# Attention and a two-layer product on one core: a first token range of 640 and all token blocks in pairs

## The chip, the core and the metric

The kernel runs on one core of a Trainium2 chip. A core has a matrix engine (TensorE, "PE" in the profile; its weight loads are "PEld"), a vector engine (VectorE, "DVE"), a scalar engine with activation functions (ScalarE, "ACT"), a general engine (GpSimd, "POOL"), and SyncE ("SP"), which here only issues DMA transfers. Each engine takes its instructions in order. The metric is the device time of one execution in microseconds (us). Three executions of the kernel before took 394.09, 394.75 and 396.04 us.

## The reference, cut to what matters

```python
# q, k, v: (8 batches, 12 heads, 448 tokens, 64); w_in: (768, 2048); w_out: (2048, 768)
scores = (1 / sqrt(64)) * q @ k.T            # per batch and head
attn = exp(scores - max(scores)); attn /= sum(attn) + 1e-9
x = attn @ v                                 # heads side by side: (3584 tokens, 768)
h = x @ w_in
g = maximum(0.01 * h, h)
out = g @ w_out                              # (3584, 768) float32
```

## The kernel before

**Units.** Two heads of one batch are a unit: u = 0 to 47, six to a batch. A unit's q, k and v are loaded (the loads of two units together, through POOL's DMA queue), cast to bf16 by POOL (`cast`; q and k into one of three `qkb` buffers, v into a ring `v_sb` of NV = 5), and q and k are transposed: by PE with a DVE copy for u < NPE = 12 (`transposes`, L248 and L254), by a DMA transposition from SP for the others (`dma_transposes`, L231). `scores` (L265) makes a chunk of 112 keys by 448 queries for two heads; ACT takes its exponential (`expo`, L274); there are four chunks a unit, 192 in all, issued in bursts of three. `rows` (L738) multiplies a whole unit's exponentials by v, the sum of weights coming from a column of ones; DVE takes the reciprocal (L744) and multiplies (L745), giving x. x is transposed into the ring `xT`, by PE for the units of the first batch (u < NXP = 6, L305), by DMA for the others (`x_transposes`).

**Ranges of tokens.** The rest, w_in, activation and w_out, goes by ranges of tokens: 384, 512, 384, 512 and so on, eight ranges cut at the multiples of 128 below the ends of the batches. Range 0 goes plainly through w_in (`plain`, L339: 16 groups of six matmuls; activation at L614) and its tokens go block by block straight through w_out (`blocks`, L586: one block kept for later, two processed). Range 1 is also plain through w_in. From range 2 on `hidden` (L449) uses seven half-size products in place of eight (sums and differences of the halves of x and w_in, and of the partial results), and from range 1 on `block_pair` (L521) does the same for two blocks of 128 tokens at a time and w_out. The sums and differences of the weights are made once, by DVE: `mix_w_in` (L371) and `mix_weights` (L350 to L357); those of x by `mix_x_part` (L396), those of the activations by `mix_h` (L421, L422).

**Order.** The order on every engine is the order in which the program emits. `place` keeps a small model of time (when PE is, when ACT is done, which of the three score slots is free) and puts bursts and rows between the groups of matmuls; how many bursts a stage gets is set by `plan`, `early` and `goals`. During the first two ranges `feed` issues, after each burst, the casts, loads and DMA transpositions that come next, and two of the four pieces of w_out; the others and those of w_in are issued by `supply` and at fixed places of the start. The loads of the weights and of the units go through the same queue, in this order. Later `advance` issues them, one of each kind per step. `mix_weights` and `mix_w_in` are generators: each `next(...)` puts one DVE operation in place.

The steps that matter below: the loads (L132, L176), the casts (L161, L163), the DMA transpositions (L231), scores (L265), rows and x (L738 to L745), the matmuls of w_in in the first range (L339), the DVE operations on the weights (L350 to L357, L371), and the blocks (L586).

Of the kernel before, what the change touches and what calls it, by code (L numbers as in the profile page):

```python
# [16 lines left out]
def kernel(  # L17
# [9 lines left out]
    nc = tc.nc  # L27
# [13 lines left out]
    cuts = [((b * S) // P) * P for b in range(B)] + [B * S]  # L41
# [10 lines left out]
    r_pool = ctx.enter_context(tc.tile_pool(name="rec", bufs=4))  # L52
# [24 lines left out]
    NV = 5  # L77
# [12 lines left out]
    NX = 4 * S  # L90
# [77 lines left out]
    for i in range(4):  # L168
        at = (slice(None), ts(i % 2, MD // 2), ts(i // 2, NW))
        w_steps.append((w_out_sb[at], w_out_v[at]))  # L170
# [56 lines left out]
    NXP = 6  # L227
    NPE = 12
# [12 lines left out]
    def transposes(u, bank=None):  # L241
        if u >= min(NPE, NU):
            return
        for parts in ((1,), (0,)) if u == 0 else ((0, 1),):
            tr = turn_tile(bank)
            for i in parts:
                for so in range(NSC):
                    nc.tensor.transpose(  # L248
                        tr[:, i, ts(so, SC)], qk_sb[u][:, i, so], ident[:SC, :SC]
                    )  # L250
            if u == 0:
                stay_warm(5)
            at = slice(parts[0], parts[-1] + 1)
            (nc.scalar.copy if u == 0 and parts == (0,) else nc.vector.tensor_copy)(  # L254
                qkT[u % NQ][:, :QL].rearrange("p (i s) -> p i s", i=2)[:, at], tr[:, at]
            )
# [39 lines left out]
    def x_transposes(u, bank=None):  # L296
        b, hp = divmod(u, HP)
        at = b * S % NX
        dst = xT[:, hp, at:at + S]
        if u >= NXP:  # L300
            turn(dst, x_t.pop(u).rearrange("p so h d -> p (so h d)"))
            return
# [28 lines left out]
    def part(i, m, kks, bank=None):  # L331

        n = cuts[i + 1] - cuts[i]
        at = cuts[i] % NX
# [9 lines left out]
    def mix_weights():  # L344
# [3 lines left out]
        for lo, hi in pieces:  # L348
            t2, t3, t4 = (w_mix[:, x, lo] for x in range(3))
            nc.vector.tensor_sub(t3, w_out_sb[:, hi, right], w_out_sb[:, lo, right])  # L350
            yield
            nc.vector.tensor_add(t2, t3, w_out_sb[:, lo, left])
            yield
            nc.vector.tensor_sub(t4, w_out_sb[:, hi, left], t2)
            yield
        for lo, hi in pieces:
            nc.vector.tensor_sub(w_out_sb[:, lo, right], w_out_sb[:, lo, right], w_out_sb[:, lo, left])  # L357
            yield
# [24 lines left out]
    def mix_x_part(i, ks):  # L383

        at = cuts[i] % NX
# [13 lines left out]
    def spots(i):  # L399

        n = cuts[i + 1] - cuts[i]
        if n == 4 * P:
            return 0, [(0, 2), (1, 3)]
        if i == 0:
            return 2, []
        return (0, [(0, 1), (KEEP, 2)]) if i % 4 == 2 else (2, [(2, 3)])

    def token(i, x):

        if x == KEEP:  # L410
            return cuts[i - i % 4] + 2 * P
        return cuts[i] + (x - spots(i)[0]) * P
# [11 lines left out]
    def hidden(i):  # L424
# [3 lines left out]
        at = cuts[i] % NX  # L428
# [75 lines left out]
    def block_pair(i, c):  # L504
# [30 lines left out]
        keep(o1, left, b, nc.scalar.copy if c == 0 and (short or i + 1 == B) else nc.vector.tensor_copy)  # L535
# [39 lines left out]
    def blocks(i, todo):  # L575

        o = {}
        for c, w in todo:
            if c not in o:
                o[c] = o_pool.tile([P, DM], F32, name="o")  # L580
            ps = next_bank()
            nw = w.stop - w.start
            for m in range(MD):
                if m == MD // 2:
                    yield MD // 2 * nw, False
                nc.tensor.matmul(  # L586
                    ps[:, :nw], h[:, m, ts(c, P)], w_out_sb[:, m, w],
                    start=(m == 0), stop=(m == MD - 1),
                )
            nc.vector.tensor_copy(o[c][:, w], ps[:, :nw])  # L590
            t0 = token(i, c)
            if w.stop == DM:
                store(o.pop(c), t0)
            yield MD // 2 * nw, True

    def plain(i, sums):

        n = cuts[i + 1] - cuts[i]
        start = spots(i)[0]
        hs = h[:, :, start * P:start * P + n]  # L600
        ready = []
        if i == 0:
            for m in opened:
                part(i, m, (KD - 1,))
        for x in range(MD):
            m = x if i == 0 else x // 2 + x % 2 * MH
            if i > 0 and x == 0:
                for y in (m, m + MH):
                    part(i, y, range(KD - 1))
            if i > 0 and x < 2:  # L610
                part(i, m, (KD - 1,))
            elif m not in opened or i > 0:
                part(i, m, range(KD))
            nc.scalar.activation(hs[:, m], open_t.pop(m)[:, :n], AX.Prelu, alpha=0.01)  # L614
            settle()
            if i == 0:
                if m == opened[-1]:
                    slots.append(idle)
                if m > MD // 2:
                    next(sums)  # L620
            else:
                if ready:
                    mix_h(i, ready.pop())
                if x % 4 == 3:
                    ready.append(x // 2 - 1)
                next(sums)
            yield n
        if ready:
            mix_h(i, ready.pop())
# [295 lines left out]
```

## Time and profile before

| | us |
|---|---|
| median of three executions (394.09 to 396.04) | 394.75 |
| the profiled execution: its own time | 394.7 |
| its span, first to last instruction | 392.8 |
| PE busy in the span | 379.9 (97%) |
| ACT busy | 262.4 (67%) |
| DVE busy | 222.0 (57%) |
| POOL busy | 143.7 (37%) |
| moved by DMA | 47.76 MB, 122 GB/s in the mean |

The durations used in this document come from the profiled execution, whose time lies 0.05 us under the median; 1.9 us of it lie around the span. A matmul's busy time in the profile is longer than the distance to the next one, since matmuls overlap; where PE is full, the distance between starts is what counts. "Releaser" is what an engine's idle time ended with. The row of tenths shows the busy share in 40 equal slices, 9.8 us each.

### The profile page before, as it was taken

The page shows a single profiled execution, that of the slowest core. Times are in us where ns is not written, and L with a number is a line of the kernel's source. Part 1 is how long each engine was busy: PE and PEld are TensorE (multiplying, and loading weights), DVE is VectorE, ACT ScalarE, POOL GpSimd, SP SyncE. Part 2 cuts the span into 40 slices and gives each one's busy share as a digit, 9 for nine tenths or more (in the row PEclk, how much of TensorE's full clock was granted, in tenths as well). Part 3 has the DMA queues.
Part 4 walks back from the last instruction along what each step waited for, and adds up shares of the span by engine and source line. Part 5 has one row for each costly group of instructions (what it writes and reads, how often), then busy time and mean ns, then how long its engine had stood idle before and what let it go on. Part 6 is the DMA issues. An engine that isn't in the chain of part 4 may idle for free.

```text
span 392.8 us, 9958 instructions
## 1 busy us (share of the span) xinstructions
PE 379.9 (97%) x4060; PEld 255.0 (65%) x4060; DVE 222.0 (57%) x476; ACT 262.4 (67%) x401; POOL 143.7 (37%) x222
## 2 busy tenths in 40 slices
PE   7999997699999999999999999999999999999996
PEld 3666664255456598556975569669856696668854
DVE  3662442277567557573475645665746457473754
ACT  5998765367767758776777767877776678608700
POOL 8787643567544433574412355052103000000000
PEclk9999999899999999999999999999999999999999
DMA  8999999999978895999872889549017420131022
GB/s 131 196 200 205 197 179 189 124 201 157 139 108 137 145 162 98 103 209 141 158 94 47 158 124 183 75 102 180 3 31 156 99 67 2 55 89 57 2 73 88
DMA packets 99325, 47.76 MB, mean 122 GB/s; under 512 B 55888, under 2 KB 95952, under 8 KB 99280
## 3 DMA queue, kind: packets, MB, share of 16 engines
q0 software_dynamic: 40272, 22.58, 44.6%
q1 hardware_dynamic: 58944, 24.53, 31.4%
q8 instruction: 31, 0.51, 0.5%
q14 instruction: 14, 0.11, 0.1%
q10 hardware_dynamic: 64, 0.02, 0.0%
HBM read 45.61 MB, written 11.01 MB: 144 GB/s over the span
## 4 chain that ended last, share of the span: by engine, by line
PE 80%; DMA 13%; POOL 5%; issue 1%; DVE 1%; POOLq 0%; DVEq 0%
PE g L521 31%; PE g L449 12%; PE sc L449 12%; PE sc L738 10%; PE sc L265 8%; DMA fv<-in_v_dram 6%; PE g L339 5%; DMA qkT<-qkb 3%; DMA w_mix<-in_v_dram 2%; DMA w_in_mix<-in_v_dram 2%; POOL v L163 1%; PE g L586 1%; POOL w_in_mix L132 1%; POOL qkb L161 1%; POOL w_mix L132 1%
## 5 line engine op out<-in xcount | busy, mean ns | idle before, releaser
L274 ACT ACTIVATE e<-sc 112x896 bf16<-112x896 f32 x192 | 163.1, 920 | 51.2 <-PE sc L265 51.2
L521 PEld LDWEIGHTS <-h 128*128 128x128 bf16 x632 | 57.3, 98 | 44.4 <-issue 12.3
L521 PE MATMUL g<-w_out_sb,h 128*128 128x384 bf16 x416 | 77.7, 326 | 0.0
L265 PE MATMUL sc<-qkT 64*128 64x448 bf16 x384 | 49.7, 353 | 6.9 <-DMA qkT<-qkb 5.7
L161 POOL COPY qkb<-fq 112x512 bf16<-112x512 bf16 x38 | 28.4, 748 | 73.9 <-DMA qkT<-qkb 53.4
L438 ACT ACTIVATE h<-c 128x384 bf16<-128x384 f32 (+1 forms) x72 | 40.6, 575 | 22.0 <-DVE c L464 15.0
L449 PEld LDWEIGHTS <-w_in_sb 128*128 128x128 bf16 x576 | 52.0, 98 | 3.9
L738 PEld LDWEIGHTS <-e 112*128 112x128 bf16 x1344 | 46.4, 98 | 9.0 <-ACT e L274 6.9
L738 PE MATMUL sc<-v,e 112*128 112x65 bf16 x1344 | 49.9, 194 | 0.0
L163 POOL COPY v<-fv 112x512 bf16<-112x512 bf16 x38 | 24.6, 652 | 62.5 <-PE sc L738 33.5
L449 PEld LDWEIGHTS <-w_in_mix 128*128 128x128 bf16 x432 | 39.1, 98 | 2.4
L744 DVE RECIPROCAL rec<-sc 112x8 f32<-112x8 f32 x42 | 8.7, 207 | 55.9 <-PE sc L738 55.8
L521 PE MATMUL g<-w_mix,h 128*128 128x384 bf16 (+1 forms) x208 | 38.7, 323 | 0.0
L339 PE MATMUL g<-xT,w_in_sb 128*128 128x512 bf16 (+1 forms) x180 | 37.9, 355 | 0.0
L526 DVE COPY o<-g 128x384 f32<-128x384 f32 x47 | 26.0, 554 | 18.5 <-PE g L521 17.8
L265 PEld LDWEIGHTS <-qkT 64*128 64x128 bf16 x384 | 14.8, 94 | 33.0 <-issue 19.1
L161 POOL COPY qkb<-fk 112x512 bf16<-112x512 bf16 x38 | 24.5, 645 | 21.2 <-DMA fk<-in_k_dram 18.9
L745 DVE TENSOR_TENSOR x<-sc,rec 112x512 bf16<-112x512 f32 x42 | 29.0, 691 | 1.5
L529 DVE TENSOR_TENSOR o<-o,g 128x384 f32<-128x384 f32 x39 | 21.4, 550 | 13.6 <-PE g L521 13.5
L339 PEld LDWEIGHTS <-w_in_sb 128*128 128x128 bf16 x192 | 17.1, 98 | 17.8 <-issue 4.3
L449 PE MATMUL g<-xT,w_in_sb 128*128 128x192 bf16 (+1 forms) x216 | 26.6, 259 | 0.0
L449 PE MATMUL sc<-xT,w_in_sb 128*128 128x192 bf16 (+1 forms) x216 | 26.6, 259 | 0.0
(94 smaller groups left out, 460.0 us busy)
## 6 DMA issues: line engine op xcount, KB each, us to landing
fq<-in_q_dram POOLq DMA_DIRECT2D x19, 224.0 KB, 5.9
fk<-in_k_dram POOLq DMA_DIRECT2D x19, 224.0 KB, 6.3
fv<-in_v_dram POOLq DMA_DIRECT2D x19, 224.0 KB, 6.2
w_in_sb<-in_moe_w_in_dram POOLq DMA_DIRECT2D x4, 768.0 KB, 11.2
w_out_sb<-in_moe_w_out_dram POOLq DMA_DIRECT2D x4, 768.0 KB, 15.8
out_dram<-o SPq DMA_DIRECT2D x7, 336.0 KB, 5.0
out_dram<-o SPq DMA_DIRECT2D x8, 288.0 KB, 3.8
out_dram<-o SPq DMA_DIRECT2D x7, 240.0 KB, 3.1
```

What stands on the lines that cost most here:

```text
L161: by(qk_sb[u][:, x].rearrange("p so h d -> p h so d"), f)
L163: by(v_sb[u % NV][:, :, :, :D], f)
L265: nc.tensor.matmul(ps[:, j, :S], t[j * D:(j + 1) * D, S + c * SC:S + c * SC + P], t[j * D:(j + 1) * D, :S], start=True, stop=True,)
L274: nc.scalar.activation(e[:, :, c, :], sc_t.pop((u, c))[:SC, :, :S], AX.Exp, scale=scale)
L339: nc.tensor.matmul(open_t[m][:, :n], w_in_sb[:, kk, ts(m, P)], xT[:, kk, at:at + n], start=(fresh and kk == kks[0]), stop=(kk == KD - 1),)
L438: nc.scalar.activation(hs[:, m:m + 2, cols], x.rearrange("p (m t) -> p m t", m=2), AX.Prelu, alpha=0.01)
L449: nc.tensor.matmul(ps[:, j * nh:(j + 1) * nh], w[:, kk, ts(j, P)], x[:, kk], start=(first and j == 0 and kk == 0), stop=(kk == KH - 1), sk ...
L521: nc.tensor.matmul(ps[:, cols], x[:, m], w[:, m], start=(first and m == 0), stop=(m == MH - 1), skip_group_check=True,)
L526: by(o[:, at], ps[:, :NW])
L529: nc.vector.tensor_add(o[:, at], o[:, at], ps[:, :NW])
L738: nc.tensor.matmul(ps[:, j, qc, :], e[:, at:at + P], vt[:, j, c, :], start=(c == 0), stop=(c == NSC - 1),)
L745: nc.vector.tensor_mul(x_t[u].rearrange("p q j d -> p j q d"), ps[:SC, :, :, :D], rec.to_broadcast([SC, 2, NSC, D]))
```

## The change

The ranges become 640, 512, 512, 512, 512, 384 and 512, seven instead of eight. The first range goes through w_in in two parts before any of it goes through w_out: `head`, the 448 tokens of the first batch, as `plain` did, and `neck`, the 192 tokens behind them, two column groups of w_in to one bank. With that all five blocks of the range have their activations; four of them go through w_out in two pairs at once, and the fifth is kept and paired in the range of 384. All 28 blocks so go in pairs; the plain `blocks` is gone. The second range, 512 tokens, already goes through w_in by the half products.

What moves with it: the DVE operations on w_out begin in the last quarter of the head (`next(outs)` from group 12) and go on in the neck and the first pair; those on w_in begin with group 5. The pieces of w_out are cut differently (4 of 16 row blocks at full width) and issued behind the loads of units 12 and 13 and the following ones; w_in's second to fourth pieces are issued somewhat later. NPE goes from 12 to 14. The x of units 10 and 11 is transposed on PE, when a score slot is free (`settle_x`), that of units 6 to 9 by DMA. The ring of x has 15 blocks of 128 instead of 4 times 448 tokens, so the x of batch 3 (units 18 to 23) lies over its end, and takes four DMA transpositions per unit there. `v_sb` has 4 buffers instead of 5, `rec` 3 instead of 4, for the room. `place` gives q/k transposes on PE a step of their own (`to["pe"]`), and may put them ahead of a burst that is due soon. At the start the two copies of unit 0's transposed q and k change between ACT and DVE. In the diff "..." marks what is left out.

```diff
-    cuts = [((b * S) // P) * P for b in range(B)] + [B * S]
+    cuts = [0, 640, 1152, 1664, 2176, 2688, 3072, B * S]
+    NR = len(cuts) - 1
+    HEAD = S
+    need = [HP * -(-t // S) for t in cuts]
...
-    NV = 5
+    NV = 4
...
-    NX = 4 * S
+    NX = 15 * P
+
+    def place_of(t):
+        return (t + NX - cuts[3]) % NX
...
-        at = (slice(None), ts(i % 2, MD // 2), ts(i // 2, NW))
-        w_steps.append((w_out_sb[at], w_out_v[at]))
+        w_steps.append([t[:, ts(i // 2 + 2 * (i % 2), MD // 4)] for t in (w_out_sb, w_out_v)])
...
-    NXP = 6
-    NPE = 12
+    NPE = 14
...
-        at = b * S % NX
+        at = place_of(b * S)
+        if bank is None:
+            x = x_t.pop(u).rearrange("p so h d -> p so (h d)")
+            if at + S <= NX:
+                turn(xT[:, hp, at:at + S], x.rearrange("p so n -> p (so n)"))
+                return
+            fit, rest = divmod(NX - at, SC)
+            turn(xT[:, hp, at:at + fit * SC], x[:, :fit].rearrange("p so n -> p (so n)"))
+            nc.sync.dma_start_transpose(out=xT[:, hp, NX - rest:], in_=x[:rest, fit])
+            nc.sync.dma_start_transpose(out=xT[:, hp, :SC - rest], in_=x[rest:, fit])
+            turn(xT[:, hp, SC - rest:at + S - NX], x[:, fit + 1:].rearrange("p so n -> p (so n)"))
+            return
         dst = xT[:, hp, at:at + S]
-        if u >= NXP:
-            turn(dst, x_t.pop(u).rearrange("p so h d -> p (so h d)"))
...
-        for lo, hi in pieces:
-            t2, t3, t4 = (w_mix[:, x, lo] for x in range(3))
-            nc.vector.tensor_sub(t3, w_out_sb[:, hi, right], w_out_sb[:, lo, right])
-            yield
-            nc.vector.tensor_add(t2, t3, w_out_sb[:, lo, left])
-            yield
-            nc.vector.tensor_sub(t4, w_out_sb[:, hi, left], t2)
-            yield
-        for lo, hi in pieces:
-            nc.vector.tensor_sub(w_out_sb[:, lo, right], w_out_sb[:, lo, right], w_out_sb[:, lo, left])
-            yield
+        for todo in (pieces[:2], pieces[2:]):
+            for lo, hi in todo:
+                t2, t3, t4 = (w_mix[:, x, lo] for x in range(3))
+                nc.vector.tensor_sub(t3, w_out_sb[:, hi, right], w_out_sb[:, lo, right])
+                yield
+                nc.vector.tensor_add(t2, t3, w_out_sb[:, lo, left])
+                yield
+                nc.vector.tensor_sub(t4, w_out_sb[:, hi, left], t2)
+                yield
+            for lo, hi in todo:
+                nc.vector.tensor_sub(w_out_sb[:, lo, right], w_out_sb[:, lo, right], w_out_sb[:, lo, left])
+                yield
...
+            return 0, [(0, 1), (2, 3)]
+        return 0, [(0, 2), (1, 3)] if cuts[i + 1] - cuts[i] == 4 * P else [(0, 1), (KEEP, 2)]
...
+    def head(ins, outs):
+
+        for m in opened:
+            part(0, m, (KD - 1,))
+        for m in range(MD):
+            if m not in opened:
+                part(0, m, range(KH))
+                yield KH * HEAD / 2400, False
+                part(0, m, range(KH, KD))
+            nc.scalar.activation(h[:, m, :HEAD], open_t.pop(m)[:, :HEAD], AX.Prelu, alpha=0.01)
             settle()
-            if i == 0:
-                if m == opened[-1]:
-                    slots.append(idle)
-                if m > MD // 2:
-                    next(sums)
+            if m == opened[-1]:
+                slots.append(idle)
+            if 5 <= m < 13:
+                next(ins)
+            if m >= 12:
+                next(outs)
+            yield (KH if m not in opened else 1) * HEAD / 2400, True
+
+    def neck(outs):
+
+        n = cuts[1] - HEAD
+        at = place_of(HEAD)
+        ms = [x + y for x in range(0, MH, 2) for y in (0, MH)]
+        held = {}
+
+        def part2(m, kks):
+            fresh = m not in held
+            if fresh:
+                held[m] = next_bank()
+            for j in range(2):
+                for kk in kks:
+                    nc.tensor.matmul(
+                        held[m][:, j * n:(j + 1) * n], w_in_sb[:, kk, ts(m + j, P)], xT[:, kk, at:at + n],
+                        start=(fresh and j == 0 and kk == 0), stop=(kk == KD - 1), skip_group_check=True,
+                    )
+
+        for m in ms[:2]:
+            part2(m, range(KD - 1))
+        yield 4 * (KD - 1) * n / 2400, False
+        for x, m in enumerate(ms):
+            if x < 2:
+                assert rows_done >= need[1], rows_done
+                settle_x()
+                part2(m, (KD - 1,))
             else:
-                if ready:
-                    mix_h(i, ready.pop())
-                if x % 4 == 3:
-                    ready.append(x // 2 - 1)
-                next(sums)
-            yield n
-        if ready:
-            mix_h(i, ready.pop())
+                part2(m, range(KH))
+                yield 2 * KH * n / 2400, False
+                part2(m, range(KH, KD))
+            nc.scalar.activation(
+                h[:, m:m + 2, HEAD:cuts[1]], held.pop(m)[:, :2 * n].rearrange("p (m t) -> p m t", m=2), AX.Prelu, alpha=0.01
+            )
+            settle()
+            if m >= MH:
+                mix_h(0, m - MH)
+            for _ in range((1, 1, 1, 1, 0, 2, 2, 2)[x]):
+                next(outs)
+            yield 2 * (KH if x > 1 else 1) * n / 2400, True
 
     def supply(u):
 
-        for what, n in {0: [('qk', 2), ('qk', 3), ('v', 1), ('v', 2), ('load', 6)], 1: [('qk', 4), ('v', 3), ('w', 1)], 2: [('qk', 5), ('v', 4), ('v', 5), ('load', 8)], 3: [('qk', 6), ('v', 6), ('w', 1)], 4: [('qk', 7), ('v', 7), ('w', 1)], 5: [('qk', 8), ('v', 8), ('load', 10), ('w', 1)]}[u]:
+        for what, n in {0: [('qk', 2), ('qk', 3), ('v', 1), ('v', 2), ('load', 6)], 1: [('qk', 4), ('v', 3), ('load', 8)], 2: [('qk', 5), ('v', 4), ('w', 1)], 3: [('qk', 6), ('v', 5), ('w', 1)], 4: [('qk', 7), ('v', 6), ('load', 10)], 5: [('qk', 8), ('v', 7), ('w', 1), ('load', 12)]}[u]:
...
+        if u in X_PE:
+            owed_x.append((u, model["now"] + 2.0))
+        else:
+            x_transposes(u)
...
+    X_PE = (HP + 4, HP + 5)
+    owed_x = []
+
+    def settle_x(now=None):
+        while owed_x and (now is None or owed_x[0][1] <= now and model["free"].get(id(slots[0]), 0.0) <= now + 0.05):
+            model["free"][id(slots[0])] = model["now"] + 1.0
+            model["now"] += 0.3
+            x_transposes(owed_x.pop(0)[0], next_slot()[:, 0])
+
...
+    def fetch():
+        for x, y in enumerate(("cast", "cast", "v")):
+            u = to["load"][x]
+            if u <= ahead and u - 3 < to[y]:
+                load_soft(u, 2, (x,))
+                to["load"][x] += 2
...
-            load(u + 5 + r)
-            to["load"] = [max(x, (u + 7 + r) // 2 * 2) for x in to["load"]]
-            load_w({9: 1, 10: 1}.get(g, 0))
+            ahead = u + 5 + r
+            fetch()
+            load_w({9: 1, 10: 1, 12: 1, 13: 1}.get(g, 0))
         if r > 0:
             dma_transposes(u + 2 + r)
-            if u + 2 + r >= NPE:
-                to["turn"] = u + 3 + r
-
-    plan = [0, 8, 8, 8, 4, 8, 4, 0]
+            to["turn"] = max(to["turn"], u + 3 + r)
+
+    plan = [8, 8, 8, 8, 8, 5, 0]
...
+            u = to["pe"]
+            if full and max(want, soon) > done and u <= min(last, NPE - 1) and state == 0:
+                transposes(u)
+                to["pe"] += 1
+                state = 1
+                model["now"] += 0.45
+                continue
...
+                if i == 0 and x % 2:
+                    next(outs if c == 0 and x in (3, 5) else ins if x > 4 else iter(()), None)
...
+    ins, outs = mix_w_in(), mix_weights()
+    early = [1, 2, 4, 6, 7, 9, 11]
+    goals = [1, 3, 5]
     groups, done = 0, 0
-    for n in plain(0, sums):
-        groups += 1
-        model["now"] += KD * n / 2400
-        model["act"] = max(model["act"], model["now"]) + 0.5
-        done += place(0, sum(x <= groups for x in early) - done, first=True, lazy=True)
+    for steps, aims, cost in ((head(ins, outs), early, 0.55), (neck(outs), goals, 0.5)):
+        groups = 0
+        base = len(early) if aims is goals else 0
+        for used, full in steps:
+            model["now"] += used
+            if full:
+                groups += 1
+                model["act"] = max(model["act"], model["now"]) + cost
+            soon = base + sum(x <= groups + 1 for x in aims) - done if full else 0
+            done += place(0, base + sum(x <= groups for x in aims) - done, soon, first=True, lazy=True, full=full, keen=NU if aims is goals or groups > 13 else 0)
...
+    second(0)
+    for _ in ins:
         pass
-    for i in range(2, B):
+    for _ in outs:
+        pass
+    for i in range(1, NR):
```

## The prediction

> **What bounds the kernel now.** I read the page's slices first, then the table by stretches, then the timeline of TensorE (PE) for its gaps, then the chain of waits ahead of them. The page:
>
> ```profile
> span 392.8 us, 9958 instructions
> ...
> PE   7999997699999999999999999999999999999996
> ...
> PEclk9999999899999999999999999999999999999999
> ```
>
> Only the slices from 59 to 79 us fall short; the rest is full. By stretches (us from:to, then the length, then each engine's busy time, granted clock, share of the DMA engines, GB/s):
>
> ```profile
> 25.94:55.14 29.20, 29.16 (x353) 18.17 (x350) 12.85 (x28) 23.93 (x37) 18.98 (x28) 1.00 1.34 200
> 55.14:78.37 23.23, 17.48 (x153) 9.30 (x152) 5.65 (x12) 9.65 (x13) 10.44 (x17) 0.93 1.23 154
> ...
> 139.85:388.00 248.15, 248.15 (x2613) 179.38 (x2611) 147.01 (x306) 164.10 (x268) 59.50 (x92) 1.00 0.57 98
> ```
>
> The plain range through w_in (first row) and everything behind 88 us run at PE's pace; the token blocks that go straight through w_out (second row) do not. What stops PE there (start, duration, in brackets the idle time before and its releaser):
>
> ```profile
> 65.11 0.74 PE L265 MATMUL sc<-qkT 64*128 64x448 bf16 x6 [2.80 <-DMA qkT<-qkb]
> ...
> 72.83 0.55 PE L265 MATMUL sc<-qkT 64*128 64x448 bf16 x4 [2.95 <-DMA qkT<-qkb]
> 73.31 4.45 PE L586 MATMUL g<-w_out_sb,h 128*128 128x384 bf16 x16
> ...
> 84.06 0.36 PE L265 MATMUL sc<-qkT 64*128 64x448 bf16 x2 [0.39 <-DVE x L745]
> ```
>
> Two waits for a transposition of q and k by DMA, and then 16 matmuls in 4.45 us instead of the 2.60 us that 15 of them take at 59.71: the granted clock fell after the second wait. Behind both stands the queue of loads that POOL issues (start, duration, what):
>
> ```profile
> 33.60 10.00 DMA fv<-in_v_dram
> ...
> 45.62 12.13 DMA fv<-in_v_dram
> 57.75 0.05 issue
> ...
> 61.68 11.10 DMA qkT<-qkb
> 72.78 0.05 issue
> 72.83 0.55 PE sc L265 x4
> 73.38 4.38 PE g L586 x16
> ```
>
> A load of 224 KB waits 10 to 12 us in that queue, and the transpositions share the DMA engines with it: for xT between 36 and 58 us "DMA to landing us min/median/max: 7.3/7.8/10.4", for qkT between 50 and 80 us 3.0/8.0/11.1.
>
> **What goes.** The waits 2.80, 2.95 and 0.39, and the slow clock: 16 matmuls in 4.45 against 2.77 (2.60 for 15 and one more start of 0.163), 1.68. Sum 7.8 us.
>
> **PE's own work.** A matmul of 384 columns starts every 0.163 us, one of 512 every 0.217 (6 in 1.30), so 0.4245 ns a column. Columns before: 96x384 + 96x512 (plain ranges), 504x192 + 504x256 (half products through w_in), 64x384 (blocks straight through w_out), 728x384 (13 pairs): 615,936. After: 96x448 + 96x192 (head and neck), 168x192 + 840x256, 784x384 (14 pairs): 609,792. That is 6,144 fewer, -2.6 us. Two more units have q and k transposed on PE, 16 matmuls at 0.06 = +0.96, and units 10 and 11 their x, 8 at 0.053 (four start within 0.16 before the last one's 0.21) = +0.42. Scores (55 bursts) and rows (42) stay. Net -1.2 to -1.3. With what goes: -9.1 us, if nothing came in its place.
>
> **What comes: the load queue and VectorE (DVE) at the end of the head.** DVE runs in order. In the new text mix_weights begins in the last quarter of the head; its first operation reads w_out pieces 1 and 2. These are now issued behind the loads of units 12 and 13. What the queue must move up to there is what it moves before up to the v of units 12, 13: four pieces of w_in, two of w_out, units 0 to 13. That landed at 57.75. Before it, q landed 52.97 and k 54.34, so v was 2.0 late against its neighbours' 1.4; a transposition of q and k was issued at 55.60 there, which the change does on PE. Bounds 55.7 (one more load of 1.4) and 57.75; I take 56.4, as most of that lateness has its cause removed.
>
> PE gets to the third score of the burst behind the rows of unit 9 at 25.94 (same first matmul of w_in) plus 84 matmuls of 448 columns at 0.19 (16.0), 46 scores at 0.111 (5.1), five units' transposes at 0.48 (2.4), four rows at 1.03 (4.1), two half rows at 0.62, two x at 0.21: 55.2 to 55.5. Its slot is freed by the multiplication of those rows, which stands on DVE behind that first operation: 0.94 + 0.21 + 0.69 after the landing, by these rows (duration, mean ns):
>
> ```profile
> L745 DVE TENSOR_TENSOR x<-sc,rec 112x512 bf16<-112x512 f32 x11 | 7.6, 691 | 0.4
> ...
> L354 DVE TENSOR_TENSOR w_mix<-w_out_sb,w_mix 128x768 bf16<-128x768 bf16 x4 | 4.0, 1008 | 0.2
> L350 DVE TENSOR_TENSOR w_mix<-w_out_sb 128x768 bf16<-128x768 bf16 x4 | 3.8, 940 | 0.0
> ```
>
> 56.4 + 1.84 = 58.2 against 55.4: **stall A, 2.8 us** (2.1 to 4.2).
>
> The x of unit 9 goes by DMA, issued at 58.2 when its multiplication is done. SP has nothing ahead of it. At 7.4 (the low half of the xT row; two earlier ones are down) it lands at 65.6. The neck's first matmul that reads it comes 5.0 us of PE work after the held score (12 matmuls 2.3, two rows 2.1, the rest 0.6): 63.2. **Stall B, 2.4 us** (1.7 if A is gone, 5.4 at 10.4).
>
> **The neck.** From there to the second product of the first pair PE has 14.9 us of work, DVE 17.6: three times 0.94 + 0.63 + 1.01 of mix_weights, two w_out differences of 0.55, four mix_h of 0.67 + 0.56, two qkT copies of 0.62, two rows of 0.90, two x copies of 0.39. PE waits for DVE at the qkT copies (bank and scores) and at a third score's slot: 2.7 by the difference of work, and about 1.1 for the times when DVE itself waits, mix_h for the activation of 0.5 to 0.6 us twice. **Stalls C, 3.8** (1.5 if only the copies wait in turn, 6 if w_mix operations take the 1.5 us that single ones of them took in before).
>
> **The rest.** At the start two small matmuls go and two copies swap ACT and DVE; PE waits there anyway (22.81 busy of the first 25.94 us), so nothing. Behind the neck all is pairs and half products, as in the row 139.85:388.00, which is full with ACT busy 164.10 of 248.15: ACT stays cover enough for the 512 ranges. The ring of v with 4 buffers instead of 5 holds POOL's v casts back; POOL is busy 59.50 of 248.15 there, so it has the time to follow. Batch 3's x wraps around the ring of 15 blocks and takes four transpositions a unit instead of one, 18 more SP issues of 1.2 us; those x are wanted a stage later, so nothing, and up to +1 without that cover. POOL's casts of units 15 and 16 wait for the landings of 14 and 15 (the slower rival). The stores of the first blocks move from 75 us to about 95, behind x and qkT transpositions on SP; nothing waits for them but the three output buffers, nothing.
>
> **Sum.** -9.1 + 2.8 + 2.4 + 3.8 = -0.1. The profiled execution took 394.7 (span 392.8 and 1.9 around it), 0.05 under the median of 394.75, so no correction: **394.6 us**.
>
> **A rule weighed.** Stalls A and B are each about as long as the wait of 2.80 that left the clock alone and the one of 2.95 that dropped it; I take no drop and keep 1.7 each for the range. "TensorE: Matmul & The Clock Gate" of the Trainium skill (Part 1, The HAM clock gate) says that an idle window of about 3.4 us, free-running, halves the clock, and under HAM oscillation that there must be no gaps over about 3.4. By it neither A nor B costs more than itself, and the slow clock at 73 us wouldn't have come at 2.95; the row differs from the rule, and by the row the sum could be 1.7 to 3.4 higher, 396.3 to 398.0, by the rule 394.6.
>
> **Rivals.**
> 1. *Faster.* The second piece of w_out is down before DVE asks (by 53.6 = 55.4 - 1.84). A is gone, B 1.7, DVE's lead makes C 1.5 to 2.5: 394.7 - 9.1 + 3.7 = 389.3. For it: the queue's slow spell at 54 to 58 coincides with three transpositions (issued 49.48, 55.60, 56.87), two of which change. Against: four loads and a piece of weights (3.7 each) have to come 2.1 to 4 us earlier from a queue that shows 200 GB/s throughout.
> 2. *Slower.* A chain through one buffer: the cast copies of units 14, 15 and 16 fall to the same one of the three qkb buffers, so cast, transposition by DMA and cast follow each other. Issue of 14 at 60.5, two casts of 1.4 (0.75 + 0.65, the page's L161 rows), three transpositions of t: 16 is down at 63.3 + 3t, and PE wants it at about 91.6. It decides from t = 9.4. The issues of before give 9.5 and 11.1 with the queue full, 3.0, 6.6 and 4.7 behind. At 11.1 the stall is 5.0: 399.6; loads of 18 and 19 behind the waiting cast on POOL would be late too. Against: the second and third fall behind 70 us, where the queue had emptied.
> 3. *The change does what is wanted of it nearly free:* A, B and C hidden, 385.6. The order of DVE's operations forbids it.
>
> **How the numbers follow.** A measurement of this kernel tells about 0.5%, 2 us, from no change (392.8 to 396.7). The forecast gets 0.52, its own range 391.5 (W 55.7, C 1.5) to 398 (W 57.75, one clock drop, C 5); of it a fifth lies under 392.8, a sixth over 396.7. The faster rival 0.30, from 387 to 391.5, with the third in its tail; the slower 0.18. Faster 0.30 + 0.10 = 0.40, same 0.33, slower 0.18 + 0.09 = 0.27. The range leaves out a tenth at each end: 388.8 to 399.0.
>
> **What would show it.** A: a wait of 2 to 4 us on scores near 56 us with DVE's x of L757 as releaser and, on DVE, L364 waiting for w_out. B: part of the neck waiting for DMA xT near 63. C: several waits of 1 to 2 us for DVE between 66 and 86. From 90 us on PE must be full; the last matmul lies near 389. The forecast is wrong if the loads land in another order, if DVE's work in the neck hides behind ACT, or if PE waits for qkT near 91.

## The result and the profile after

The changed kernel takes 414.19 us (median; 413.6 to 414.3), the kernel before 394.68 beside it: a ratio of 1.0486, interval 1.0457 to 1.0515. That is 19.5 us slower, where the forecast was 394.6 and its range ended at 399.0.

The page of the changed kernel, its span and its slices of 10.3 us:

```profile
span 411.8 us, 9991 instructions
...
PE   8999976779979999599999999999999999999996
...
PEclk9999998699999999979999999999999999999999
```

PE falls short from 51 to 93 us, as the forecast had it in kind, but also near 113 to 124 and at 165 to 175, where the forecast had it full. The granted clock, which fell once before, falls in three places. The timeline of TensorE (start, duration, in brackets the idle time before and its releaser):

```profile
59.40 0.36 PE L270 MATMUL sc<-qkT 64*128 64x448 bf16 x2 [1.90 <-DVE x L757]
...
68.20 1.56 PE L616 MATMUL g<-xT,w_in_sb 128*128 128x192 bf16 x17 [2.02 <-DMA xT<-x]
...
70.45 0.32 PE L616 MATMUL g<-xT,w_in_sb 128*128 128x192 bf16 x2 [0.48 <-DVE xT L319]
71.35 0.55 PE L253 MATMUL g<-ident,qkb 112*128 112x112 bf16 x8 [0.58 <-ACT h L633]
72.69 0.74 PE L270 MATMUL sc<-qkT 64*128 64x448 bf16 x6 [0.79 <-DVE qkT L259]
...
75.30 0.91 PE L253 MATMUL g<-ident,qkb 112*128 112x112 bf16 x8 [1.60 <-ACT h L633]
...
92.72 0.36 PE L270 MATMUL sc<-qkT 64*128 64x448 bf16 x2 [2.80 <-DVE x L757]
...
119.56 0.81 PE L530 MATMUL g<-w_out_sb,h 128*128 128x384 bf16 x4 [2.39 <-DVE o L535]
...
169.94 0.36 PE L270 MATMUL sc<-qkT 64*128 64x448 bf16 x2 [0.81 <-DMA qkT<-qkb]
174.46 1.44 PE L530 MATMUL g<-w_out_sb,h 128*128 128x384 bf16 x4 [4.16 <-DVE o L535]
175.69 1.97 PE L750 MATMUL sc<-v,e 112*128 112x65 bf16 x32
```

The first two are stalls A and B, the next four and the 2.80 are C. All have the kind of place that the forecast gave; the 2.80 comes later than its 66 to 86 us. The 2.39 and 4.16 are in no step of the forecast. The last line is the clock: 32 matmuls of rows in 1.97 us that take 1.19 elsewhere. The three slow stretches in the table by stretches (us from:to, length, then PE's and the others' busy time; the third figure from the end is the granted clock):

```profile
60.00:64.00 4.00, 4.00 (x42) 2.68 (x40) 1.50 (x3) 1.35 (x2) 3.28 (x6) 0.57 1.17 207
74.00:81.00 7.00, 5.70 (x38) 4.47 (x37) 2.80 (x7) 3.40 (x7) 3.91 (x7) 0.52 0.36 52
173.00:180.00 7.00, 5.54 (x44) 3.54 (x44) 3.62 (x10) 0.00 (x0) 1.80 (x3) 0.52 0.71 85
```

The clock was at half for 3.41, 6.83 and 6.83 us. Half of PE's busy time in these stretches, 1.7, 2.8 and 2.8 us, is the most that they can have cost; the same groups at full clock, by the distances between starts, make it about 1.5, 2.7 and 2.6. I take 1.7, 2.7 and 2.7, 7.1 together, against 1.7 before.

What stood behind 2.39 and 4.16 shows on DVE, whose idle time ended with a transposition by DMA:

```profile
113.16 0.56 DVE L535 COPY o<-g 128x384 f32<-128x384 f32 x1 [0.92 <-PE g L530]
117.03 0.80 DVE L410 TENSOR_TENSOR x_mix<-xT 128x512 bf16<-128x512 bf16 x1 [3.31 <-DMA xT<-x]
...
118.97 0.54 DVE L535 COPY o<-g 128x384 f32<-128x384 f32 x1
...
165.58 0.55 DVE L535 COPY o<-g 128x384 f32<-128x384 f32 x1
173.06 0.42 DVE L410 TENSOR_TENSOR x_mix<-xT 128x512 bf16<-128x512 bf16 x1 [6.93 <-DMA xT<-x]
...
173.86 0.55 DVE L535 COPY o<-g 128x384 f32<-128x384 f32 x1
```

DVE stood 3.3 and 6.9 us at the sums of x for the next range (mix_x_part, L410), because x had not landed; behind it in DVE's order stood the copy of a product (L535) whose bank PE needed. And why x was late the second time, from SP's queue:

```profile
157.85 1.19 SPq L236 DMA_TRANSPOSE xT<-x  x1
159.09 1.22 SPq L311 DMA_TRANSPOSE xT<-x  x1
160.35 1.93 SPq L312 DMA_TRANSPOSE xT<-x  x1
162.33 1.23 SPq L236 DMA_TRANSPOSE xT<-x  x1
163.67 2.39 SPq L331 DMA_DIRECT2D out_dram<-o  x4
166.17 3.11 SPq L236 DMA_TRANSPOSE qkT<-qkb  x2
169.37 1.19 SPq L236 DMA_TRANSPOSE xT<-x  x1
```

One unit of batch 3 holds SP for 5.7 us (157.85 to 163.56), then come stores and q/k transpositions; the next unit's x, ready at 161.8 when DVE's multiplication ended, is issued from 169.37 on, and the last one's, ready at 165.7, from 174.47 on.

The accounts, to the end of the last matmul (389.2 before, 407.9 after, +18.65): waits of more than 0.15 us behind the first matmul 20.9 against 7.85 (+13.1), slow clock 7.1 against 1.7 (+5.4). Without these two, 379.7 us are left before and 379.9 after: the 1.25 us that PE's own work was to fall by do not show, or small delays took them back.

### The profile page after: what moved, and what is told of

The parts are those of the page before. It is cut to its first block, busy times and chain, and to the rows that moved or that the text cites. A ratio compares the mean times of both kernels' runs of the same rounds, so it can differ in the third digit from the quotient of the medians.

```text
span 411.8 us, 9991 instructions
## 1 busy us (share of the span) xinstructions
PE 385.3 (94%) x4074; PEld 263.2 (64%) x4074; DVE 229.5 (56%) x486; ACT 264.8 (64%) x391; POOL 142.2 (35%) x222
## 4 chain that ended last, share of the span: by engine, by line
PE 79%; DMA 8%; DVE 5%; SPq 3%; issue 2%; ACT 1%; POOL 1%; DVEq 0%; ACTq 0%; POOLq 0%
PE g L530 27%; PE g L458 13%; PE sc L458 13%; PE sc L750 9%; PE sc L270 7%; DMA xT<-x 6%; PE g L352 3%; PE g L616 2%; DMA w_in_mix<-in_k_dram 2%; PE g L289 2%; SPq L236 2%; PE g L253 1%; POOL w_in_mix L139 1%; DVE x L757 1%; DVE o L535 1%
## 5 line engine op out<-in xcount | busy, mean ns | idle before, releaser
L530 PEld LDWEIGHTS <-h 128*128 128x128 bf16 x680 | 62.0, 98 | 55.6 <-issue 22.4
L530 PE MATMUL g<-w_out_sb,h 128*128 128x384 bf16 x448 | 86.6, 330 | 7.3 <-DVE o L535 7.3
L447 ACT ACTIVATE h<-c 128x512 bf16<-128x512 f32 (+1 forms) x72 | 43.5, 611 | 24.0 <-DVE c L473 15.4
L458 PEld LDWEIGHTS <-w_in_sb 128*128 128x128 bf16 x576 | 54.7, 98 | 6.6 <-issue 0.7
L530 PE MATMUL g<-w_mix,h 128*128 128x384 bf16 (+1 forms) x224 | 41.9, 327 | 0.0
L535 DVE COPY o<-g 128x384 f32<-128x384 f32 x53 | 29.2, 552 | 13.0 <-PE g L530 12.5
L458 PE MATMUL g<-xT,w_in_sb 128*128 128x256 bf16 (+1 forms) x216 | 28.5, 268 | 0.3 <-DVE o L538 0.3
L458 PE MATMUL sc<-xT,w_in_sb 128*128 128x256 bf16 (+1 forms) x216 | 28.5, 268 | 0.0
L470 ACT COPY c<-g 128x512 f32<-128x512 f32 (+1 forms) x12 | 6.8, 569 | 31.6 <-PE g L458 26.6
L530 PE MATMUL g<-w_mix,hmix 128*128 128x384 bf16 x112 | 21.5, 327 | 0.0
```

The source lines that it names most:

```text
L447: nc.scalar.activation(hs[:, m:m + 2, cols], x.rearrange("p (m t) -> p m t", m=2), AX.Prelu, alpha=0.01)
L458: nc.tensor.matmul(ps[:, j * nh:(j + 1) * nh], w[:, kk, ts(j, P)], x[:, kk], start=(first and j == 0 and kk == 0), stop=(kk == KH - 1), sk ...
L530: nc.tensor.matmul(ps[:, cols], x[:, m], w[:, m], start=(first and m == 0), stop=(m == MH - 1), skip_group_check=True,)
L535: by(o[:, at], ps[:, :NW])
```

## The experiments

The theory after the result: (W) four DMA transpositions a unit fill SP's queue in batch 3; (A, B, D) in the first range DVE's work on w_out and the x of unit 9 come late; (X) the sums of x ask too early. The rival to all of them: the places only show that the queue of loads, or the lateness of the first 90 us, holds everything. Ratios are to the kernel before, run beside each; its median was 394.14 beside e1 to e4, 393.59 beside e5 to e8, 394.07 beside e9 and e10 and 395.15 beside e11, so differences of medians across these groups are good to about 1 us.

**e1_one_turn: the wrap taken away.** Another layout of the same ring; each range half is still in one piece.

```diff
     def place_of(t):
-        return (t + NX - cuts[3]) % NX
+        return t + 8 * P if t < 2 * S else t - 2 * S if t < 6 * S else t - 6 * S
...
-        one, two = slice(at, at + nh), slice(at + nh, at + 2 * nh)
+        to_two = place_of(cuts[i] + nh)
+        one, two = slice(at, at + nh), slice(to_two, to_two + nh)
```

> The changed kernel with another layout of the x ring: the same 15 blocks, but tokens 896 to 2687 lie from column 0, tokens 0 to 895 from column 1024, and the last 896 from column 0 again, so that no batch lies over the ring's end and each unit of batch 3 takes one DMA transposition instead of four. Theory W (the four transpositions fill SP's queue between 122 and 182 us, x lands late, mix_x on DVE waits for it and holds the copies that PE waits for): the waits of 0.81 and 4.16 at 170 to 174 us and the slow clock behind them (about 2.7) go, 414.2 - 7.7 = 406.5, between 405 and 408. Rival V (SP is crowded there by output stores and q/k transpositions anyway, or the stage inherits its lateness from the first 90 us): 412 to 414, the waits stay.

405.9 us, 1.0314 (1.0272 to 1.0355): 8.3 us off the changed kernel by the medians, 6.8 by the two ratios. Where PE stood for 4.16 us it now runs through (TensorE, same place in the order):

```profile
167.89 0.74 PE L270 MATMUL sc<-qkT 64*128 64x448 bf16 x6
168.56 0.82 PE L532 MATMUL g<-w_out_sb,h 128*128 128x384 bf16 x4
169.33 1.20 PE L752 MATMUL sc<-v,e 112*128 112x65 bf16 x32
```

DVE's wait for xT between 120 and 182 us fell from 10.2 to 0.2, and no slow clock is left behind 82 us. Theory W holds; the waits of the first 124 us are all still there (2.24, 1.64, 3.45, 2.80, 2.59), so the 4.16 and the slow clock behind it were not inherited from them.

**e4_before_4turns: the wrap's price alone, in the kernel before.**

```diff
-            turn(dst, x_t.pop(u).rearrange("p so h d -> p (so h d)"))
+            x = x_t.pop(u).rearrange("p so h d -> p so (h d)")
+            if b == 3:
+                turn(xT[:, hp, at:at + 2 * SC], x[:, :2].rearrange("p so n -> p (so n)"))
+                nc.sync.dma_start_transpose(out=xT[:, hp, at + 224:at + 320], in_=x[:96, 2])
+                nc.sync.dma_start_transpose(out=xT[:, hp, at + 320:at + 336], in_=x[96:, 2])
+                turn(xT[:, hp, at + 336:at + 448], x[:, 3:].rearrange("p so n -> p (so n)"))
+                return
+            turn(dst, x.rearrange("p so n -> p (so n)"))
```

> The kernel before with the x of batch 3 (units 18 to 23) taken into the ring by four DMA transpositions a unit, cut as the change cuts them, in place of one; nothing else. Theory W (18 more issues of 1.2 us on SP, and the order behind them, are dear by themselves): x late at the end of that stage, 398 to 403. Rival V (the cover that I assumed holds, and it takes the change's tighter order to lose it): 394 to 396.

398.48 us, 1.0113 (1.0085 to 1.0141), 4.3 us slower. TensorE of this kernel, one wait that the kernel before doesn't have, and DVE ahead of it:

```profile
143.54 0.66 PE L456 MATMUL sc<-x_mix,w_in_mix 128*128 128x192 bf16 x6
147.18 0.66 PE L456 MATMUL g<-xT,w_in_sb 128*128 128x192 bf16 x6 [2.98 <-DVE c L471]
```

```profile
145.98 0.69 DVE L752 TENSOR_TENSOR x<-sc,rec 112x512 bf16<-112x512 f32 x1 [3.51 <-DMA xT<-x]
```

Its place is another (half products of the next range), and so is the link: DVE's multiplication of a unit's rows (L752) waited 3.51 us for a transposition, the last of a unit's four, issued at 140.48 and down at 145.86. The kernel has three buffers for x, and this wait is for one that was still being read. Behind it stood the sum (L471) that PE needed. What is the same is that DVE, in order, is held by transpositions that are late on SP. The cost doesn't need the change's tighter order, though it is larger there.

**e2_mix_later: stall A alone.**

```diff
-            if m >= 12:
+            if m >= 13:
                 next(outs)
...
-            for _ in range((1, 1, 1, 1, 0, 2, 2, 2)[x]):
+            for _ in range((2, 1, 1, 1, 0, 2, 2, 2)[x]):
```

> The changed kernel with the first DVE operation on w_out (the one that waits for the second piece of w_out) one group of matmuls later, behind the multiplication of unit 9's rows, and two such operations instead of one at the neck's first group. Theory A (DVE, held by the landing, holds that multiplication, with it PE's third score and the transposition of unit 9's x): the wait of 1.90 at 59.4 goes, the wait of 2.02 for xT at 68.2 falls to under 1.5, the slow clock of 60 to 64 us (1.7) goes: 409 to 411. Rival D (DVE has more to do in the neck than PE, so what is moved comes back as waits for DVE between 70 and 93 us): 412.5 to 415.

413.75 us, 1.0495 (1.0438 to 1.0552), no different from the change. The time is that of rival D, its mechanism is not. TensorE:

```profile
57.32 0.74 PE L270 MATMUL sc<-qkT 64*128 64x448 bf16 x6
...
66.55 2.88 PE L616 MATMUL g<-xT,w_in_sb 128*128 128x192 bf16 x17 [3.56 <-DMA xT<-x]
```

The third score no longer waits; the 1.90 is gone and stall B has grown from 2.02 to 3.56. The transposition of unit 9's x was issued 2.05 us earlier (57.32 for 59.37) and landed only 1.65 earlier (66.51 for 68.16): 9.2 us under way, while PE asked for it 3.2 earlier (62.99 for 66.18). Stall A was cover for stall B. Both theories had missed that. The clock was at half for 13.65 us there (65.7 to 79.4), where the change has 3.41 and 6.83.

**e5_no_mix: DVE's work on w_out left out** (on the ring of e1_one_turn).

```diff
-        t2, t3, t4 = (w_mix[:, x] for x in range(3))
+        t2, t3, t4 = (w_out_sb[:, lo, :NW] for x in range(3))
...
-                nc.vector.tensor_sub(t3, w_out_sb[:, hi, right], w_out_sb[:, lo, right])
                 yield
-                nc.vector.tensor_add(t2, t3, w_out_sb[:, lo, left])
                 yield
...
```

> The ring of e1_one_turn, and mix_weights left out: DVE makes none of the 16 sums and differences of w_out, and the half products take a half of w_out itself in their place (the same matmuls, shapes and DMA, but not the reference's product). It prices that DVE work where the change puts it. Theory A with D (the waits for DVE at 59 and 92 us are this work's, the first by waiting for w_out, the second by its length): 2.24 and 2.80 go, most of the 1.64 for xT, and the slow clock of 59 to 63 us (1.7): 405.9 - 8 = 398, between 397 and 400. Rival L (PE is held by the loads and transpositions, DVE only shows it): 403 to 406, waits for DMA in their place.

402.77 us, 1.0225 (1.0198 to 1.0252): 3.1 of the expected 8. The 2.80 at 92 us went, so that wait hangs on this work; stall B took over stall A again:

```profile
66.05 2.28 PE L613 MATMUL g<-xT,w_in_sb 128*128 128x192 bf16 x17 [3.54 <-DMA xT<-x]
```

and the clock stayed at half from 66.7 to 80.4. In the neck the loads and transpositions hold PE, not DVE alone: part of rival L.

**e6_x9_pe: the x of unit 9 on PE** (on the ring of e1_one_turn).

```diff
-    X_PE = (HP + 4, HP + 5)
+    X_PE = (HP + 3, HP + 4, HP + 5)
```

> The ring of e1_one_turn, and the x of unit 9 transposed on PE like those of units 10 and 11, not by DMA. Theory B (the neck waits for that DMA transposition): the wait of 1.64 for xT at 67 us goes, four small matmuls come (0.2): 404 to 405; if the slow clock of 73 to 80 us hangs on the sum of the waits there, up to 2.8 more, 401.5. Rival C (DVE's copy, behind the same work on w_out, comes no earlier, or the next wait in the neck takes it over): 405.5 to 407.

401.5 us, 1.0189 (1.0164 to 1.0213), 4.4 less than e1_one_turn, the far end of theory B. The wait for xT is gone, the slow stretch of 6.8 us is down to one of 3.4, that at 60 us is gone, another of 3.4 came at 112.9, and the 2.80 at 92 is gone too, as rows, x copies and sums of w_out came in another order. What stayed and what grew, on TensorE:

```profile
59.69 0.37 PE L318 MATMUL sc<-ident,x 112*128 112x112 bf16 x4 [2.61 <-DVE x L759]
...
112.22 0.85 PE L532 MATMUL g<-w_mix,hmix 128*128 128x384 bf16 x4 [3.01 <-DVE o L537]
```

**e7_sums_later: the sums of x later in the first pairs** (on the ring of e1_one_turn).

```diff
-                    if fresh[y] > 4 and next(todo, 0) is None:
+                    if fresh[y] > (4 if i else 9) and next(todo, 0) is None:
```

> The ring of e1_one_turn, and in the first pairs the sums of x for the second range (mix_x_part) begin five half products later after the last rows than in the change. Theory X (DVE, in order, waits there for the x of unit 16, issued at 111.9 behind stores and other transpositions on SP, and with it the copy that PE needs): the wait of 2.59 at 119 us goes, 403 to 404. Rival T (the half products of the second range need these sums at once, so the wait comes back some us later): 405 to 406.5.

404.8 us, 1.0273 (1.024 to 1.0306). The wait of 2.59 is gone and only 0.41 came later, so rival T falls. But the intervals of this kernel and e1_one_turn overlap: in this kernel's profile w_out landed at 55.7, stall A was absent, B was 3.50 and the slow clock ran from 69 to 79.5 and from 93 to 96.5. It also ran from 11 to 18 us, far ahead of the edit, so that w_in began at 27.9 us where it began at 25.0 in the profile of e1_one_turn. Alone, this run does not price the wait.

**e9_three: the edits of e1_one_turn, e6_x9_pe and e7_sums_later together.**

> Three edits together on the changed kernel: the ring of e1_one_turn, the x of unit 9 on PE (e6_x9_pe) and the later sums of x (e7_sums_later). Theory of separate causes: what e6_x9_pe left at 112 us, 3.01 for DVE behind mix_x, and the slow clock behind it, 1.7, go: 401.5 - 4.7 = 396.8, between 395.5 and 398. Rival (a time given back elsewhere, as with e7_sums_later alone, which gained 1): 400 to 401.5.

398.23 us, 1.0089 (1.0055 to 1.0123): 3.3 less than e6_x9_pe, 1.4 short of the expected. Nothing above 0.5 us is left behind 88 us; here the sums of x do have their price.

**e10_four: and e2_mix_later's edit on top.**

> The three edits of e9_three and the first DVE operation on w_out one group later (e2_mix_later). With x of unit 9 on PE no DMA transposition stands behind that multiplication any more. Theory A: the wait of 2.61 at 59.7 us now really goes, 396.8 - 2.6 = 394 (393 to 395), so that the change with its four misplaced waits mended is back at the kernel before. Rival D: DVE's operations come later into the neck and PE waits there: 396 to 398.

396.0 us, 1.0049 (1.0023 to 1.0075): 2.2 less. Without a transposition by DMA behind it, stall A is real, and ends with that edit. What is left in the neck, on TensorE:

```profile
67.95 0.37 PE L318 MATMUL sc<-ident,x 112*128 112x112 bf16 x4 [1.10 <-DVE x L759]
68.87 0.32 PE L618 MATMUL g<-xT,w_in_sb 128*128 128x192 bf16 x2 [0.55 <-DVE xT L319]
69.78 0.91 PE L253 MATMUL g<-ident,qkb 112*128 112x112 bf16 x8 [0.58 <-ACT h L635]
...
71.47 1.30 PE L270 MATMUL sc<-qkT 64*128 64x448 bf16 x6 [0.47 <-DVE qkT L259]
```

and a slow stretch of 6.8 us behind them (granted clock 0.50 from 69.1 to 75.9, PE busy 5.75, so up to 2.9 lost). The profile is of the slowest of ten executions (397.73), which has a second slow stretch at 11 to 18 us. The change with its misplaced waits mended is 1.9 us slower than the kernel before. The slow clock alone doesn't explain that: the one execution of the ten whose granted clock was 1.0 took 395.85.

**e3_before_npe14 and e8_before_x11: the change's transpositions on PE, alone, in the kernel before.** First NPE alone:

```diff
-    NPE = 12
+    NPE = 14
```

> The kernel before with NPE = 14 alone: q and k of units 12 and 13 transposed on PE instead of by DMA. Theory N (the two waits of before at 65 and 73 us belong to these two transpositions alone): 2.80, 2.95 and the slow clock of 1.7 go, 16 small matmuls come for 0.96: 388.3, between 387.5 and 389.5. Rival S (the queue of loads holds the next transpositions back in the same way, so the waits pass to units 14 and 15): 392 to 395.

392.45 us, 0.996 (0.9939 to 0.9981): faster, by less than theory N. The waits for q and k of units 12 and 13 went (0.66 for q and k is left at 72.86, and 0.59 for w_out came at 66.87), and a long one came, on TensorE:

```profile
73.16 2.33 PE L339 MATMUL g<-xT,w_in_sb 128*128 128x512 bf16 x9
78.13 0.58 PE L339 MATMUL g<-xT,w_in_sb 128*128 128x512 bf16 x1 [2.64 <-DMA xT<-x]
```

It passed not to units 14 and 15 but to the x of unit 11, computed at 67.3 and issued by SP at 71.22, behind the transposition of unit 14 that was itself issued at 69.89. This profile is of the slowest of ten executions (394.03); four of the ten had a granted clock of 1.0 and took 391.6 to 392.3, so the median holds the slow clock behind that wait only in part. So:

```diff
-        if u >= NXP:
+        if u >= NXP and u != 11:
...
-        x_transposes(u)
+        if u != 11:
+            x_transposes(u)
...
     assert done == len(early), done
+    assert rows_done == 12, rows_done
+    x_transposes(11, next_bank())
```

> The kernel before with NPE = 14 (e3_before_npe14), and the x of unit 11 transposed on PE behind the token blocks, not by DMA behind a q/k transposition on SP. Theory Q (the wait of 2.64 for xT and the slow clock behind it, 1.7, are what keeps e3_before_npe14 from the full 6.5 us): 392.45 - 4.2 = 388 to 389.5. Rival S (the full load queue holds something else in the same place): 391.5 to 393.

389.88 us, 0.9898 (0.9878 to 0.9918): 2.6 less than e3_before_npe14, 0.4 above the end of theory Q's range and 1.6 under rival S. TensorE between 60 and 84 us, all its waits there:

```profile
72.38 0.36 PE L265 MATMUL sc<-qkT 64*128 64x448 bf16 x2 [0.66 <-DMA qkT<-qkb]
72.68 0.37 PE L305 MATMUL g<-ident,x 112*128 112x112 bf16 x4
...
78.57 0.37 PE L265 MATMUL sc<-qkT 64*128 64x448 bf16 x2 [0.39 <-DVE x L745]
```

and in this execution the clock is full from 20 us to the last matmul. It beats both kernels: two units' q and k and one unit's x off the DMA queues, and nothing else of the change.

**e11_before_warm: the clock by itself.**

```diff
         for a, c in todo:
+            if (a, c) == (13, 0):
+                for _ in range(7):
+                    nc.tensor.matmul(banks[0], warm[:, :P], warm, start=True, stop=True)
             scores(a, c)
```

> The kernel before, with seven matmuls of zeros (512 columns, about 1.5 us, into a bank that is free) in the wait of 2.95 us for q and k of unit 13, ahead of the score that waits; nothing else moves. Theory H (the clock falls when PE idles for more than half of a fixed window of 3.41 us: the idle share of the window before the slow one was 66% in the profile before, and falls to under 40%): the wait shrinks to about 1.5 but ends at the same moment, the slow stretch of 74 to 77.5 us is gone, and the time falls by 1.7: 392.4 where the kernel before takes 394.1. Rival K (the clock goes by something else than idle time in such a window): the slow stretch stays, 394 to 394.5.

394.54 us, 0.9993 (0.9966 to 1.002), the time of rival K; for the mechanism inconclusive. In its profile the wait at the place of the added matmuls is gone and the clock stays full there; but the earlier wait, 2.80 before, was 4.31 in this execution and lowered the clock instead (from 65.4 to 68.8):

```profile
65.72 1.30 PE L265 MATMUL sc<-qkT 64*128 64x448 bf16 x6 [4.31 <-DMA qkT<-qkb]
...
71.88 1.69 PE L758 MATMUL g<-x_mix 128*128 128x512 bf16 x6
```

The two waits are 2.80 and 2.95 in the profile before and 4.31 and nothing in this one, so they vary by about as much as the 1.7 us sought.

## Why the prediction was wrong

- **What goes, and PE's own work** (-9.1): right in kind, not shown in size. The two long waits for q and k are gone; the 1.25 of PE's work do not show in the accounts. What the two waits are worth without the rest of the change is 4.0 us (3.2 to 4.8, from the interval of e8_before_x11), where 7.4 less 1.2 for the added transposes on PE would have been 6.2; a wait of 0.66 is left, and the rest is not accounted for.
- **Stall A, 2.8**: 1.90, at the place and with the releaser named; w_out landed at 57.82 (56.4 taken, 57.75 the bound), and the head ran 2 us longer than counted, which I had not allowed for; the two errors partly cancel, so the size of A is in part luck. **Stall B, 2.4**: 2.02. That A hides B, so that mending A alone is worth nothing, was not in the sum (e2_mix_later).
- **Stalls C, 3.8**: 3.45 and 2.80, 6.25, just over the upper bound of 6. The 2.80 lies at a third score's slot, as the text had it, though at 92.7 us and not before 86, and goes with the DVE work (e5_no_mix). Of the other four waits 2.18 were for ACT's activation and not for DVE.
- **The rule weighed: "I take no drop"**: failed. The clock dropped after A and in the neck, 1.7 and 2.7 us. I had compared single gaps; ahead of the neck's drop stand waits of 0.58, 0.79 and part of 1.60 us, 1.85 together within 3.41 us, with no gap over 1.6 among them. The range kept 1.7 for each of A and B, and its upper end only one drop. The rule of the Trainium skill ("TensorE: Matmul & The Clock Gate", HAM oscillation) that there must be no gaps over about 3.4 us is too mild for the same rows: these two drops came behind 1.90 and 1.85 us of idle time in 3.41 us.
- **"The rest": the step that failed most.** "Those x are wanted a stage later, so nothing, and up to +1 without that cover" was measured at 8.3 us by e1_one_turn (6.8 by the ratios) and at 4.3 in the kernel before by e4_before_4turns. I had counted the 18 issues of 1.2 us but not where SP's order puts them: in front of stores and q/k transpositions and of the next unit's x. Nor are they wanted a stage later: the 320 first tokens of batch 3 belong to the range that comes next, and its sums are taken at the end of this stage. With the 7.7 us of that place the sum would have been 402.
- **"Behind the neck all is pairs and half products, full"**: 2.39 at 119.56 was missed. The second range now goes by half products, so its sums of x stand at the end of the first pairs, where x of units 16 and 17 has just been issued. In the kernel before that range was plain. e9_three against e6_x9_pe prices this at 3.3 us with its slow clock.
- **The rivals.** The slower one, a chain of casts through one buffer, came as a chain (POOL's cast for unit 15 began at 72.97, when transposition 14 had landed at 72.92) but cost PE no wait: transposition 14 took 11.7 us (61.22 to 72.92), 15 and 16 only 2.9 each, the queue being empty by then, as the text had it against. The faster one asked for w_out earlier and had B at 1.7 without A; where w_out did land earlier and A was absent (55.71 in the profile of e7_sums_later), B was 3.50.

Put together: 394.6 with 7.7 for the wrap, 2.7 for the sums at 119, 4.4 for two clock drops, 2.5 for C and -1.3 for A and B gives 410.6; of the 3.6 left to 414.2, 2 lie in the longer head. From its first matmul of w_in (25.89) to the wait of the third score (57.50) PE took 31.6 us where 29.3 to 29.6 had been counted. Of that, 0.97 are three waits for ACT (0.36, 0.24 and 0.37); the 84 matmuls of 448 columns took 16.8 by the distances between starts, not 16.0, and the 46 scores 5.9, not 5.1. The last 1.6 are about the 1.25 of PE's work that does not show; where it went stays open.

## What to carry to other kernels

A queue that issues DMA is an engine with an order: an added issue is to be priced at the place where it stands, with what is issued behind it and when the last one's data is read, not by its own time. Of waits in a row, the next is to be worked out as if the first were gone: here the first was only the second's cover. And a stage that stands between the landing of its data and the next stage needs a row of its own in the sum, even where the kernel before was full there, if the change moves the reader earlier.

## What the runs showed of the hardware

The clock goes by the idle time in fixed windows of 3.41 us, not by the longest gap. The windows come out of the clock's own record: in all thirteen traces the slow stretches up to the last matmul last 3.41, 6.83, 10.24 or 13.65 us where there are any, and the stretches at full clock between them are whole multiples of 3.41 us too (10.24 and 92.16 in the changed kernel), so that every change lies on one grid. Two such windows of the changed kernel, both at full clock (PE's busy time is the second figure of the row):

```profile
70.83:74.24 3.41, 1.57 (x16) 0.80 (x16) 0.98 (x3) 1.56 (x3) 1.27 (x3) 1.00 1.10 145
87.89:91.31 3.42, 2.03 (x20) 0.97 (x17) 3.21 (x6) 2.12 (x4) 3.11 (x4) 1.00 0.25 48
```

The first holds 1.85 us of idle time in short waits, and the clock was at half behind it. The second holds half of the single wait of 2.80 us, 1.38 us, the next window 1.42, and the clock stayed full. Behind 26 us, windows at full clock with 0.9 to 1.76 us of idle time were followed by full clock, those with 1.85 us and more by half clock. The exceptions: 1.58 and 1.65 (e9_three and e10_four) were followed by half clock, in windows that also held x transposes on PE, and 1.90 at the very end of e8_before_x11 by full clock. At the start 1.24 and 1.26 dropped the clock in e10_four and e7_sums_later, while 1.25 in e2_mix_later did not, so idle time is not all of it. Once the clock is down, 0.83 us and more in a window kept it down for another (0.40 did too, at the start), 0.39 and less let it rise: 1.06 and 1.24 us are why the drops of 74 and 173 us lasted 6.83 us. The idle times are worked out from PE's records, whose ends are partly modelled, and no run changed the idle time of a window alone (e11_before_warm was meant to).

A DMA transposition costs SP the same whatever its size: 1.22 us for a piece of 96 or 16 rows, 1.23 for the large pieces (medians between 120 and 182 us). And its way to landing goes with what the DMA engines carry beside it. In the changed kernel it was 8.8 to 11.7 us for the five transpositions issued between 40 and 62 us, with weights in flight. For q and k of one unit it was 11.7 us from 61.22, at a mean busy share of the DMA engines of 1.25, and 2.9 us from 74.17, at 0.44; for x 8.8 us from 59.37, at 1.19, and 2.35 us from 84.92, at 0.25.
